# Attention and mixture-of-experts kernel: another order of loads, squares and weight splits in its opening

## The chip, the cores and the metric

The kernel runs on one core of a Trainium2 chip. The core has a matrix engine (TensorE, PE in the profile), a vector engine (VectorE, DVE), an engine for activation functions (ScalarE, ACT), a general engine (GpSimd, POOL) and a synchronisation engine (SyncE, SP) that here issues nearly all DMAs. A name with a q behind it (SPq, POOLq) is the instruction queue of that engine. The metric is the device time of one execution in microseconds.

## The reference

Two stages follow each other. The attention is linear attention with random features, and its output, with the heads put side by side, is the input of four dense experts whose outputs are summed with normalised weights:

```python
def phi(x):                                   # x: (batch 4, heads 8, seq 576, dim 64), omega: (128, 64)
    h = einsum('bhsd,md->bhsm', x, omega) - sum(x * x) / 2
    return exp(h - max(h)) / sqrt(128)
q_p, k_p = phi(q * 64**-0.25), phi(k * 64**-0.25)
kv  = einsum('bhsm,bhsd->bhmd', k_p, v)
num = einsum('bhsm,bhmd->bhsd', q_p, kv)
den = einsum('bhsm,bhm->bhs', q_p, sum_s(k_p)) + 1e-6
x   = (num / den) as (2304, 512)
p   = domain_probs / (sum(domain_probs) + 1e-9)
out = sum over e in 0..3 of p[:, e] * (relu(x @ w1[e]) @ w2[e])       # w1: 512x1024, w2: 1024x512
```

## The kernel before, in words

All is float32 at the borders. The expert matmuls split each operand into a high part in a rounded format (fp32r) and a low part that is the remainder, and use three products: high by high, low by high, high by low.

**Attention.** Heads are worked in pairs, four pairs a batch. For batch 0 (class `Pair`) a pair's keys lie as 64 rows; `square` writes their squares into the other 64 rows of the tile, so that one matmul with `om` (features above, a constant below) gives projection minus half the squared length. `project` makes it for a group of token tiles and takes the row maxima on VectorE, `exp` the exponentials on ScalarE, `sum_keys` sums keys by values into `kv` and copies it out (`kvs`), `turn` transposes the query features, `numerators` multiplies them with `kvs` and divides, `finish` transposes the result into the ring buffers `x_hi` and `x_lo`.

**Experts.** A visit is half an expert for a block of tokens. `hidden` makes four hidden tiles (128 features each) from the rings and four `w1` tiles, `relu` splits them into `hh` and `hl`, `outputs` multiplies them with four `w2` tiles and accumulates. Weights come as raw tiles of 128x512 (`wraw`, 256 KB each): `load_w` issues the next load on SP, `split_w` takes the oldest raw tile, writes its high part (on ScalarE as a rule, on GpSimd in the opening) and its low part (on GpSimd), and then calls `load_w`. A raw tile's buffer is free again once its low part is written. There are `RAWB` raw buffers.

**Order.** The kernel is written with a manual schedule: on each engine the instructions stand in the order of the code, and SP issues DMAs in that order too, so that a DMA that waits for a buffer holds all behind it.

`begin` (L452) is the opening: the first 256 tokens of batch 0 for all four pairs, staggered. While pair 0's keys are summed, pair 1's are projected, and pair 2's and 3's are being loaded and squared. Among them stand the first eight `split_w`, four for `w1` and four for `w2`, and at the end the first expert visit's `hidden`, in four parts as the pairs finish. `first_visit` (L570) does that visit's `relu` and `outputs` with eight more splits, for the second visit, and between its steps `emit` runs `first_rest` (L582), the remaining 320 tokens of batch 0. After that, `steps` runs visits with the other batches' attention between them.

Of the kernel before, what the change touches and what calls it, by code (L numbers as in the profile page):

```python
# [7 lines left out]
F32R = mybir.dt.float32r  # L8
# [6 lines left out]
def attention_moe(ctx, tc, kT, qT, kd, qd, kn, qn, vn, omT, probs, w1, w2, out):  # L15
# [10 lines left out]
    nc = tc.nc  # L26
    _, NP, D, _ = kT.shape
# [3 lines left out]
    E, FT, P, KC, _ = w1.shape  # L31
    EPS = 1e-6
    QS = float(D) ** -0.25
    RING = 1536
# [3 lines left out]
    const = ctx.enter_context(tc.tile_pool(name="const", bufs=1))  # L38
    att = ctx.enter_context(tc.tile_pool(name="att", bufs=2))
    moe = ctx.enter_context(tc.tile_pool(name="moe", bufs=1))  # L40
    psum = ctx.enter_context(tc.tile_pool(name="psum", bufs=8, space=bass.MemoryType.PSUM))

    def bank(name):
        return psum.tile([P, 512], F32, tag="ps", name=name)

    def f32(ap):
        return ap.bitcast(F32)
# [6 lines left out]
    prs = const.tile([P, NT // P], F32, name="prs")  # L54
    vas = [const.tile([P, 4, VW], F32, name=f"va{i}") for i in range(2)]
    vbs = [const.tile([P, NP, VW], F32, name=f"vb{i}") for i in range(2)]
    x_hi = const.tile([P, NP, RING], F32R, name="x_hi")
    x_lo = const.tile([P, NP, RING], F32R, name="x_lo")

    def scale_om():  # L60
        nc.vector.tensor_scalar(om[:D], om[:D], QS, None, ALU.mult)

    def normalize_probs():
        nc.vector.tensor_reduce(prs, pr, AX.X, ALU.add)
        nc.vector.tensor_scalar(prs, prs, 1e-9, None, ALU.add)
        nc.vector.reciprocal(prs, prs)
        nc.vector.tensor_tensor(pr, pr, prs[:, :, None].to_broadcast([P, NT // P, E]), ALU.mult)
# [282 lines left out]
                mine = [(256, 256)] + mine  # L350
            visits.append((u, e, hf, mine))

    W1B, W2B, RAWB, HB, AB = 6, 6, 4, 6, 7
    W = {}
    items = [(v, which, i) for v in range(len(visits)) for which in ("w1", "w2") for i in range(FH)]
    loads, splits = list(items), list(items)
# [2 lines left out]
    def load_w(eng=nc.sync):  # L359
        if not loads:  # L360
            return
        v, which, i = key = loads.pop(0)
        _, e, hf, _ = visits[v]
        f = hf * FH + i
        raw[key] = t = moe.tile([P, 512], F32, tag="wraw", name="wraw", bufs=RAWB)
        eng.dma_start(t, w1[e, f].rearrange("p k f -> p (k f)") if which == "w1" else w2[e, f * P:(f + 1) * P])

    def split_w(hi=nc.scalar, lo=nc.gpsimd):
        if not splits:
            return  # L370
        key = splits.pop(0)
        t = raw.pop(key)
        a, c = (moe.tile([P, 512], F32R, tag=key[1] + x, name=key[1] + x, bufs={"w1": W1B, "w2": W2B}[key[1]]) for x in "hl")
        if hi is nc.scalar:
            hi.activation(a, t, AF.Copy)  # L375
        else:
            hi.tensor_copy(a, t)
        lo.tensor_tensor(c, t, f32(a), ALU.subtract)  # L378
        W[key] = a, c
        load_w()  # L380
# [15 lines left out]
    def relu(ps, n):  # L396
        ha, hc = (moe.tile([P, 512], F32R, tag=x, name=x, bufs=HB)[:, :n] for x in ("hh", "hl"))
        nc.scalar.activation(ha, ps[:, :n], AF.Relu)  # L398
        nc.vector.scalar_tensor_tensor(hc, ps[:, :n], 0.0, f32(ha), ALU.max, ALU.subtract)  # L399
        return ha, hc  # L400

    def outputs(v, hs, i, t):

        _, e, hf, _ = visits[v]
        ps = bank("g2")
        ts_ = slice(t * P, (t + 1) * P)
        for c in range(FH):
            (ha, hc), (wa, wc) = hs[c], W[v, "w2", c]
            nc.tensor.matmul(ps, ha[:, ts_], wa, start=(c == 0), stop=False)  # L409
            nc.tensor.matmul(ps, ha[:, ts_], wc, start=False, stop=False)  # L410
            nc.tensor.matmul(ps, hc[:, ts_], wa, start=False, stop=(c == FH - 1))  # L411
        sc = pr[:, i, e:e + 1]
        n_tiles[i] += 1
        if n_tiles[i] == 1:
            acc[i] = moe.tile([P, DM], F32, tag="acc", name="acc", bufs=AB)
            nc.scalar.activation(acc[i], ps, AF.Copy, scale=sc)
        else:
            nc.vector.scalar_tensor_tensor(acc[i], ps, sc, acc[i], ALU.mult, ALU.add)  # L418
        if n_tiles[i] == len(HALVES):
            stores.append((i, acc.pop(i)))  # L420
# [31 lines left out]
    def begin():  # L452

        ps = [Pair(0, hp) for hp in range(NP)]
        first, rest = slice(0, 4 * P), slice(4 * P, 9 * P)
        ps[0].load("k", [first, rest])
        nc.scalar.dma_start(om[:D], omT)
        ps[0].load("q0", eng=nc.scalar)
        ps[1].load("k", [first, rest])
        nc.gpsimd.memset(om[D:], -QS * QS / 2)  # L460
        ps[1].load("q0", eng=nc.scalar)
        ps[0].load_v()
        make_identity(nc, ident)
        for t in vas[:1]:
            nc.gpsimd.memset(t[:, :, 0:VW:VW - 1], 1.0)
        for t in vbs[:1]:
            nc.gpsimd.memset(t, 0.0)
            nc.gpsimd.memset(t[:D, :, 0:1], 1.0)
            nc.gpsimd.memset(t[D:, :, VW - 1:VW], 1.0)
        ps[0].load_tails()  # L470
        ps[1].load_v()
        load_w()
        load_w()
        scale_om()

        def keys(hp):
            for g in range(3):
                ps[hp].project("k", g)

        def keys_exp(hp):  # L480
            for g in range(3):
                ps[hp].exp("k", g)

        ps[0].square("k", nc.scalar, first)
        ps[0].square("k", nc.vector, rest)
        ps[0].square("q0", nc.scalar)
        ps[1].square("k", nc.scalar, first)
        ps[1].square("k", nc.gpsimd, rest)
        nc.gpsimd.memset(vas[1][:, :, 0:VW:VW - 1], 1.0)
        keys(0)  # L490

        ps[2].load("k")
        ps[2].load("q0")
        ps[0].project("q", 0)
        ps[1].square("q0", nc.vector)
        keys_exp(0)
        keys(1)
        ps[2].square("k", nc.gpsimd, first)
        ps[2].square("k", nc.gpsimd, rest)

        ps[0].sum_keys()
        ps[2].load_v()
        ps[3].load("k")
        ps[3].load("q0")
        load_w()
        load_w()
        ps[0].exp("q", 0)
        ps[1].project("q", 0)
        keys_exp(1)
        ps[2].square("q0", nc.vector)  # L510
        keys(2)
        ps[3].square("k", nc.gpsimd, first)
        ps[3].square("k", nc.gpsimd, rest)
        nc.gpsimd.memset(vbs[1], 0.0)
        nc.gpsimd.memset(vbs[1][:D, :, 0:1], 1.0)
        nc.gpsimd.memset(vbs[1][D:, :, VW - 1:VW], 1.0)

        ps[0].turn(0, nc.vector)
        ps[1].sum_keys()
        ps[3].load_v()  # L520
        nc.sync.dma_start(pr, probs.rearrange("(i p) e -> p i e", p=P))
        ps[1].exp("q", 0)
        ps[2].project("q", 0)
        keys_exp(2)
        ps[3].square("q0", nc.vector)
        keys(3)
        for _ in range(4):
            split_w(nc.gpsimd, nc.gpsimd)
        for p in ps[:2]:
            p.load("q1")  # L530
        for j in range(2):
            nc.sync.dma_start(om_r[j * D:(j + 1) * D], omT)

        ps[0].numerators(0)
        ps[1].turn(0, nc.vector)
        ps[2].sum_keys()
        ps[2].exp("q", 0)
        ps[3].project("q", 0)
        keys_exp(3)
        for p in ps[:2]:  # L540
            p.square("q1", nc.gpsimd)
        for _ in range(4):
            split_w(nc.gpsimd, nc.gpsimd)

        ps[0].finish(0)
        ps[1].numerators(0)
        ps[2].turn(0, nc.vector)
        ps[3].sum_keys()
        ps[3].exp("q", 0)

        normalize_probs()
        nc.vector.tensor_scalar(om_r, om_r, QS, None, ALU.mult)
        ps[1].finish(0)
        ps[2].numerators(0)
        ps[3].turn(0, nc.vector)
        g1 = [bank("g1") for _ in range(FH)]
        for f in range(FH):
            hidden(0, f, 0, 256, g1[f], [0])
        ps[2].finish(0)
        ps[3].numerators(0)  # L560
        for f in range(FH):
            hidden(0, f, 0, 256, g1[f], [1])
        ps[3].finish(0)
        for f in range(FH):
            hidden(0, f, 0, 256, g1[f], [2])
        for f in range(FH):
            hidden(0, f, 0, 256, g1[f], [3])
        return ps, g1

    def first_visit(g1):  # L570
        hs = []
        for f in range(FH):
            split_w()
            hs.append(relu(g1[f], 256))
            yield 0.5
        for t in range(2):
            for _ in range(2):
                split_w()
            outputs(0, hs, t, t)
            yield 1  # L580

    def first_rest(pairs):  # L582
# [101 lines left out]
```

## Time and profile before

| | us |
|---|---|
| median of 3 runs (lowest to highest) | 975.51 (974.34 to 976.88) |
| the profiled execution | 980.6 |
| its span, first to last instruction | 978.2 |
| TensorE busy in the span | 957.4 |

The profiled execution is 5.1 us longer than the median, and 2.4 us of it lie outside the span. All that follows is read from that one execution. Times in a timeline are microseconds from the start of the span. The granted clock is a share of full speed: 1.00 is 2.4 GHz, 0.50 is 1.2 GHz, and a value between is a stretch with both.

### The profile page before, as it was taken

The page shows a single profiled execution, that of the slowest core. Times are in us where ns is not written, and L with a number is a line of the kernel's source. Part 1 is how long each engine was busy: PE and PEld are TensorE (multiplying, and loading weights), DVE is VectorE, ACT ScalarE, POOL GpSimd, SP SyncE. Part 2 cuts the span into 40 slices and gives each one's busy share as a digit, 9 for nine tenths or more (in the row PEclk, how much of TensorE's full clock was granted, in tenths as well). Part 3 has the DMA queues.
Part 4 walks back from the last instruction along what each step waited for, and adds up shares of the span by engine and source line. Part 5 has one row for each costly group of instructions (what it writes and reads, how often), then busy time and mean ns, then how long its engine had stood idle before and what let it go on. Part 6 is the DMA issues. An engine that isn't in the chain of part 4 may idle for free.

```text
span 978.2 us, 13669 instructions
## 1 busy us (share of the span) xinstructions
PE 957.4 (98%) x5216; PEld 808.6 (83%) x5216; DVE 369.2 (38%) x760; ACT 342.2 (35%) x806; POOL 371.8 (38%) x312
## 2 busy tenths in 40 slices
PE   6989999999999999999999999999999999999998
PEld 6978888887888888878888888888888888888887
DVE  3434445553334444343333354544311222222222
ACT  3345344433262324334326252434323221322120
POOL 3756543343342234444444344444414422431230
PEclk9799999999999999999999999999999999999999
DMA  6434544232432412423263342422313211221211
GB/s 152 108 107 119 171 126 135 78 111 80 126 89 80 141 48 86 145 69 90 82 202 99 112 135 76 135 78 75 109 63 86 76 34 64 87 65 31 78 33 65
DMA packets 60737, 94.09 MB, mean 96 GB/s; under 512 B 10176, under 2 KB 18560, under 8 KB 60672
## 3 DMA queue, kind: packets, MB, share of 16 engines
q1 hardware_dynamic: 60432, 92.92, 32.4%
q8 instruction: 41, 0.67, 0.3%
q10 hardware_dynamic: 240, 0.30, 0.1%
q14 instruction: 24, 0.20, 0.1%
HBM read 88.48 MB, written 4.72 MB: 95 GB/s over the span
## 4 chain that ended last, share of the span: by engine, by line
PE 94%; ACT 2%; DMA 1%; DVE 1%; POOL 1%; SPq 1%; issue 0%; POOLq 0%; ACTq 0%
PE g L392 14%; PE g L394 14%; PE g L393 14%; PE g L409 13%; PE g L411 13%; PE g L410 13%; PE kv L142 3%; PE nd L166 2%; PE qt_ps L151 2%; PE k_ps L234 1%; PE q_ps L234 1%; PE x_ps L188 1%; PE t_ps L238 1%; DMA k<-in_kT 1%; DMA va<-in_vn 1%; PE k_ps L114 1%
## 5 line engine op out<-in xcount | busy, mean ns | idle before, releaser
L378 POOL TENSOR_TENSOR w1l<-wraw,w1h 128x512 fp32r<-128x512 f32 x128 | 164.5, 1286 | 383.5 <-ACT w1h L375 374.9
L392 PE MATMUL g<-x_hi,w1h 128*128 128x512 f32 (+1 forms) x688 | 252.8, 367 | 0.0
L394 PE MATMUL g<-x_hi,w1l 128*128 128x512 f32 (+1 forms) x688 | 248.0, 360 | 0.0
L393 PE MATMUL g<-x_lo,w1h 128*128 128x512 f32 (+1 forms) x688 | 247.9, 360 | 0.0
L399 DVE SCALAR_TENSOR_TENSOR hl<-g,hh 128x512 fp32r<-128x512 f32 (+1 forms) x172 | 104.1, 605 | 345.4 <-ACT hh L398 345.4
L409 PE MATMUL g<-w2h,hh 128*128 128x512 f32 x576 | 228.4, 397 | 0.2 <-ACT hh L398 0.2
L411 PE MATMUL g<-w2h,hl 128*128 128x512 f32 x576 | 225.5, 391 | 0.0
L410 PE MATMUL g<-w2l,hh 128*128 128x512 f32 x576 | 225.0, 391 | 0.0
L398 ACT ACTIVATE hh<-g 128x512 fp32r<-128x512 f32 (+1 forms) x172 | 91.0, 529 | 375.0 <-PE g L394 374.8
L378 POOL TENSOR_TENSOR w2l<-wraw,w2h 128x512 fp32r<-128x512 f32 x128 | 163.1, 1289 | 144.0 <-ACT w2h L375 143.4
L418 DVE SCALAR_TENSOR_TENSOR acc<-g,pr,acc 128x512 f32<-128x512 f32 x126 | 94.6, 750 | 192.9 <-PE g L411 192.5
L394 PEld LDWEIGHTS g<-x_hi,w1l 128*128 128x128 f32 x688 | 131.0, 190 | 21.0
L392 PEld LDWEIGHTS g<-x_hi,w1h 128*128 128x128 f32 x688 | 131.1, 190 | 20.7 <-issue 0.5
L393 PEld LDWEIGHTS g<-x_lo,w1h 128*128 128x128 f32 x688 | 131.1, 190 | 19.5
L411 PEld LDWEIGHTS g<-w2h,hl 128*128 128x128 f32 x576 | 108.2, 188 | 24.1 <-DVE hl L399 1.1
L409 PEld LDWEIGHTS g<-w2h,hh 128*128 128x128 f32 x576 | 108.4, 188 | 23.5 <-ACT hh L398 0.7
L410 PEld LDWEIGHTS g<-w2l,hh 128*128 128x128 f32 x576 | 108.3, 188 | 21.3
L375 ACT ACTIVATE w2h<-wraw 128x512 fp32r<-128x512 f32 x124 | 76.2, 635 | 104.2 <-PE g L411 55.1
L375 ACT ACTIVATE w1h<-wraw 128x512 fp32r<-128x512 f32 x124 | 77.8, 627 | 0.1
L265 ACT ACTIVATE kp<-k_ps,nbk 128x128 f32<-128x128 f32 x96 | 27.4, 379 | 34.1 <-DVE nbk L259 34.1
L166 PEld LDWEIGHTS nd<-kvs,qt 128*128 128x128 f32 x256 | 33.9, 196 | 3.5 <-DVE qt L157 1.5
L166 PE MATMUL nd<-kvs,qt 128*128 128x65 f32 x256 | 33.0, 273 | 1.4 <-DVE qt L157 1.4
(82 smaller groups left out, 599.4 us busy)
## 6 DMA issues: line engine op xcount, KB each, us to landing
wraw<-in_w SPq DMA_DIRECT2D x256, 256.0 KB, 2.7
out<-acc SPq DMA_DIRECT2D x18, 256.0 KB, 3.2
va<-in_vn SPq DMA_DIRECT2D x16, 256.0 KB, 5.5
k<-in_kd SPq DMA_DIRECT2D x12, 288.0 KB, 3.1
q<-in_qd SPq DMA_DIRECT2D x12, 288.0 KB, 4.6
k<-in_kn SPq DMA_DIRECT2D x12, 288.0 KB, 4.9
q<-in_qn SPq DMA_DIRECT2D x12, 288.0 KB, 5.2
q<-in_qT SPq DMA_DIRECT2D x4, 160.0 KB, 3.4
```

The source lines that it names most:

```text
L166: nc.tensor.matmul(nd[:, t, cs], self.query_tile(j, 2 * part + t), self.kv[:, cs], start=True, stop=True)
L375: hi.activation(a, t, AF.Copy)
L378: lo.tensor_tensor(c, t, f32(a), ALU.subtract)
L392: nc.tensor.matmul(ps[:, :n], wa[:, w], x_hi[:, k, cs], start=(k == 0), stop=False)
L393: nc.tensor.matmul(ps[:, :n], wa[:, w], x_lo[:, k, cs], start=False, stop=False)
L394: nc.tensor.matmul(ps[:, :n], wc[:, w], x_hi[:, k, cs], start=False, stop=(k == KC - 1))
L398: nc.scalar.activation(ha, ps[:, :n], AF.Relu)
L399: nc.vector.scalar_tensor_tensor(hc, ps[:, :n], 0.0, f32(ha), ALU.max, ALU.subtract)
L409: nc.tensor.matmul(ps, ha[:, ts_], wa, start=(c == 0), stop=False)
L410: nc.tensor.matmul(ps, ha[:, ts_], wc, start=False, stop=False)
L411: nc.tensor.matmul(ps, hc[:, ts_], wa, start=False, stop=(c == FH - 1))
L418: nc.vector.scalar_tensor_tensor(acc[i], ps, sc, acc[i], ALU.mult, ALU.add)
```

## The change

Five things change.

1. The first two weight loads move behind pair 2's keys and queries in SP's order, and pair 2's keys are loaded in two pieces (512 and 640 columns) instead of one.
2. The squares of pair 2's first piece move from GpSimd to VectorE, ahead of pair 1's maxima; the second piece stays on GpSimd.
3. There are six raw weight buffers instead of four. As many loads are issued ahead as before (four), so a load no longer waits for the low part that was just issued, but for the one two splits earlier.
4. In `first_visit` each `relu` stands ahead of its split and each `outputs` ahead of its two splits, and six of the eight low parts go to VectorE (the four of `w1`, and one of two after each `outputs`).
5. `x_hi` and `x_lo` are allocated from a pool of their own behind the others.

```diff
+    xs = ctx.enter_context(tc.tile_pool(name="xs", bufs=1))
...
+    x_hi = xs.tile([P, NP, RING], F32R, name="x_hi")
+    x_lo = xs.tile([P, NP, RING], F32R, name="x_lo")
...
-    x_hi = const.tile([P, NP, RING], F32R, name="x_hi")
-    x_lo = const.tile([P, NP, RING], F32R, name="x_lo")
...
-    W1B, W2B, RAWB, HB, AB = 6, 6, 4, 6, 7
+    W1B, W2B, RAWB, HB, AB = 6, 6, 6, 6, 7
...
         ps[1].load_v()
-        load_w()
-        load_w()
         scale_om()
...
         keys(0)
-        ps[2].load("k")
+        ps[2].load("k", [first, rest])
         ps[2].load("q0")
+        load_w()
+        load_w()
         ps[0].project("q", 0)
         ps[1].square("q0", nc.vector)
         keys_exp(0)
+        ps[2].square("k", nc.vector, first)
         keys(1)
-        ps[2].square("k", nc.gpsimd, first)
         ps[2].square("k", nc.gpsimd, rest)
...
         for f in range(FH):
-            split_w()
             hs.append(relu(g1[f], 256))
+            split_w(lo=nc.vector)
             yield 0.5
         for t in range(2):
-            for _ in range(2):
-                split_w()
             outputs(0, hs, t, t)
+            split_w()
+            split_w(lo=nc.vector)
             yield 1
```

The instructions below are listed in the order in which they stand on an engine; line numbers of the changed kernel are two higher from L92 on. First SP in the opening, before: `k` of 1152 columns are pair 2's and then pair 3's keys, `q` their queries, `va` values, `wraw` weights.

```order
L94 DMA va_73<-in_vn 128x4x128
L366 DMA wraw<-in_w 128x512 x2
L90 DMA k<-in_kT 64x1152
L90 DMA q_135<-in_qT 64x512
L94 DMA va_72<-in_vn 128x4x128
L90 DMA k<-in_kT 64x1152
L90 DMA q_192<-in_qT 64x512
L366 DMA wraw<-in_w 128x512 x2
```

The same place on SP in the changed kernel:

```order
L96 DMA va_78<-in_vn 128x4x128
L92 DMA k<-in_kT 64x512
L92 DMA k<-in_kT 64x640
L92 DMA q_135<-in_qT 64x512
L368 DMA wraw<-in_w 128x512 x2
L96 DMA va_77<-in_vn 128x4x128
L92 DMA k<-in_kT 64x1152
L92 DMA q_196<-in_qT 64x512
L368 DMA wraw<-in_w 128x512 x2
```

Pair 2's keys are now directly behind pair 1's values; pair 3's keys stand where they stood, behind the values that take pair 0's buffer.

VectorE in the opening, before; `q_90` are pair 1's queries, the `nm` after it the maxima of pair 1, and the last two rows the first of pair 2.

```order
L117 TENSOR_REDUCE nm<-q_ps 128x4
L106 TENSOR_TENSOR q_90<-q_90 64x512
L117 TENSOR_REDUCE nm<-k_ps 128x4 x2
L117 TENSOR_REDUCE nm<-k_ps 128x1
L117 TENSOR_REDUCE nm<-q_ps 128x4
L106 TENSOR_TENSOR q_135<-q_135 64x512
L117 TENSOR_REDUCE nm<-k_ps 128x4 x2
```

The same place on VectorE in the changed kernel:

```order
L119 TENSOR_REDUCE nm<-q_ps 128x4
L108 TENSOR_TENSOR q_93<-q_93 64x512
L108 TENSOR_TENSOR k<-k 64x512
L119 TENSOR_REDUCE nm<-k_ps 128x4 x2
L119 TENSOR_REDUCE nm<-k_ps 128x1
L119 TENSOR_REDUCE nm<-q_ps 128x4
L108 TENSOR_TENSOR q_135<-q_135 64x512
L119 TENSOR_REDUCE nm<-k_ps 128x4 x2
```

The square of pair 2's first piece stands ahead of pair 1's maxima, which so wait for that piece's landing.

VectorE in `first_visit`, before; `g` are the four hidden tiles, `nm<-q_ps` the maxima of the remaining queries of pairs 0 and 1, `qt` the copies after `turn` of pair 0.

```order
L399 SCALAR_TENSOR_TENSOR hl<-g_485,hh 128x256
L117 TENSOR_REDUCE nm<-q_ps 128x4
L117 TENSOR_REDUCE nm<-q_ps 128x1
L399 SCALAR_TENSOR_TENSOR hl<-g_486,hh 128x256
L117 TENSOR_REDUCE nm<-q_ps 128x4
L117 TENSOR_REDUCE nm<-q_ps 128x1
L399 SCALAR_TENSOR_TENSOR hl<-g_487,hh 128x256
L399 SCALAR_TENSOR_TENSOR hl<-g_488,hh 128x256
L157 COPY qt<-qt_ps 128x512
```

The same place on VectorE in the changed kernel, from the second hidden tile on:

```order
L380 TENSOR_TENSOR w1l<-wraw,w1h 128x512
L119 TENSOR_REDUCE nm<-q_ps 128x4
L119 TENSOR_REDUCE nm<-q_ps 128x1
L401 SCALAR_TENSOR_TENSOR hl<-g_490,hh 128x256
L380 TENSOR_TENSOR w1l<-wraw,w1h 128x512
L119 TENSOR_REDUCE nm<-q_ps 128x4
L119 TENSOR_REDUCE nm<-q_ps 128x1
L401 SCALAR_TENSOR_TENSOR hl<-g_491,hh 128x256
L380 TENSOR_TENSOR w1l<-wraw,w1h 128x512
L401 SCALAR_TENSOR_TENSOR hl<-g_492,hh 128x256
L380 TENSOR_TENSOR w1l<-wraw,w1h 128x512
L159 COPY qt<-qt_ps 128x512
```

Behind each `hl` now stands a low part of `w1`, so four of them are ahead of the copies that pair 0's numerators read.

## Rows read from the trace of the kernel before

**Rows 1.** Stretches of TensorE: length, busy us (instructions), granted clock, DMA share, GB/s.
```profile
20.00:30.00 10.00, 9.50 (x46) 0.51 0.27 66
...
40.00:50.00 10.00, 10.00 (x64) 0.66 0.37 107
...
60.00:70.00 10.00, 7.17 (x38) 0.90 0.59 163
70.00:80.00 10.00, 10.00 (x74) 0.93 0.29 89
80.00:978.20 898.20, 890.62 (x4783) 1.00 0.32 94
```

**Rows 2.** Waits of TensorE, first 80 us: total us, times, longest.
```profile
PE k_ps L114 <- POOL k L106: 4.0, 2, 3.5
PE qt_ps L151 <- ACT qp L126: 2.8, 1, 2.8
```

**Rows 3.** Timeline of SP's queue, first 42 us: start, us, instruction, count.
```profile
11.05 0.98 SPq L366 DMA_DIRECT2D wraw<-in_w  x2
12.20 0.48 SPq L90 DMA_DIRECT2D k<-in_kT  x1
...
15.25 0.47 SPq L90 DMA_DIRECT2D k<-in_kT  x1
...
33.59 1.11 SPq L90 DMA_DIRECT2D q<-in_qT  x2
```

**Rows 4.** Landing times of the key loads, first 40 us.
```profile
DMA to landing us min/median/max: 2.9/5.0/6.5
```

**Rows 5.** Timeline of GpSimd, VectorE and ScalarE around pair 2's keys.
```profile
11.53 0.69 DVE L106 TENSOR_TENSOR q<-q 64x512 f32<-64x512 f32 x1
...
12.24 1.49 DVE L117 TENSOR_REDUCE nm<-k_ps 128x4 f32<-128x512 f32 x3
...
15.95 2.46 ACT L126 ACTIVATE kp<-k_ps,nm 128x128 f32<-128x128 f32 x9
...
18.13 2.69 POOL L106 TENSOR_TENSOR k<-k 64x512 f32<-64x512 f32 x2 [4.36 <-DMA k<-in_kT]
18.77 0.94 DVE L106 TENSOR_TENSOR q<-q 64x512 f32<-64x512 f32 x1 [2.36 <-DMA q<-in_qT]
...
21.88 2.25 POOL L106 TENSOR_TENSOR k<-k 64x512 f32<-64x512 f32 x2 [1.06 <-DMA k<-in_kT]
```

**Rows 6.** Timeline of TensorE, 14 to 40 us.
```profile
14.57 1.11 PE L114 MATMUL q_ps<-om,q 128*128 128x128 f32 x8
19.21 1.16 PE L114 MATMUL k_ps<-om,k 128*128 128x128 f32 x8 [3.54 <-POOL k L106]
...
24.45 3.52 PE L142 MATMUL kv<-va,kp 128*128 128x65 f32 x16
...
29.57 2.62 PE L114 MATMUL k_ps<-om,k 128*128 128x128 f32 x18
...
33.54 1.90 PE L142 MATMUL kv<-va,kp 128*128 128x65 f32 x16
...
36.44 1.00 PE L166 MATMUL nd<-kvs,qt 128*128 128x65 f32 x8
37.27 0.61 PE L151 MATMUL qt_ps<-ident,qp 128*128 128x128 f32 x4
39.15 0.49 PE L138 MATMUL kv<-vb,kp 128*128 128x130 f32 x2 [1.27 <-ACT kp L126]
```

**Rows 7.** The page's group of `w1` low parts on GpSimd.
```profile
L378 POOL TENSOR_TENSOR w1l<-wraw,w1h 128x512 fp32r<-128x512 f32 x128 | 164.5, 1286 | 383.5 <-ACT w1h L375 374.9
```

**Rows 8.** Timeline of ScalarE, 48 to 90 us.
```profile
63.66 0.63 ACT L375 ACTIVATE w2h<-wraw 128x512 fp32r<-128x512 f32 x1 [3.68 <-DMA wraw<-in_w]
...
67.26 1.40 ACT L126 ACTIVATE qp<-q_ps,nm 128x128 f32<-128x128 f32 x5
```

**Rows 9.** Timeline of SP's queue, 48 to 90 us.
```profile
60.86 7.30 SPq L366 DMA_DIRECT2D wraw<-in_w  x6
```

## Prediction

> **What bounds the kernel now.** I read TensorE by stretches first. After 80 us it is busy for 890.6 of 898.2 us at the full clock [rows 1]; none of the edits touches that work, so what they are worth lies in the first 80 us. There the reader sees two kinds of loss. The first is a lower clock: 10 x (1 - 0.51) = 4.9 us between 20 and 30, 10 x (1 - 0.66) = 3.4 between 40 and 50, and 1.0 + 0.7 = 1.7 between 60 and 80 [rows 1]. The second is waiting, read next: 4.0 us for GpSimd's squares of pair 2's keys and 2.8 for ScalarE's exponentials of pair 1's late queries [rows 2], and 1.3 for ScalarE's exponentials of pair 3's keys [rows 6]. Each fall of the clock follows one of these waits, so a wait that goes may take a low stretch with it. Last I read who was late at each wait, on the timelines.
>
> **First piece: pair 2's keys.** Their load was issued at 12.20, behind two weight loads from 11.05 [rows 3], and GpSimd could square only at 18.13 [rows 5], 5.9 us later. TensorE had ended its work before at 14.57 + 1.11 = 15.7 and started these keys at 19.21 [rows 6]. Now the load takes the weights' place at 11.05, in two pieces 0.6 apart. The traced landings are 2.9 to 6.5 us, median 5.0 [rows 4]; that gives 14.0 to 17.6 for the first piece. I take 15.0, a landing of 4: the piece is under half of the load that took 5.9, and 512 KB less stands before it. VectorE squares it in 0.69 [rows 5] to 15.7, just as TensorE is free. The second piece lands at 15.6 and takes GpSimd 640/1152 of 2.25 = 1.25 [rows 5], to 16.9; TensorE asks for it at 16.7. So the wait of 4.0 becomes about 0.2 (bounds: 0, and 2.6 if the first piece lands at 17.6).
>
> VectorE is in order, so pair 1's three maxima (1.49 from 12.24) stand behind that square, from 15.7 to 17.2. For them waits ScalarE: its exponentials of pair 1's keys started at 15.95 and took 2.46 [rows 5]; now the first maximum is there at 16.4 and they end at 18.9. TensorE comes to pair 1's key sum at 16.9 + 1.3 for ten more projections + 0.5 for a turn = 18.7. Cost 0.2.
>
> **What is late next: pair 3's keys.** Their load keeps its issue at 15.25 [rows 3], since it stands behind a values load that waits for pair 0's key sum, and the bytes ahead of it are the same. I leave its landing at 21.88. GpSimd's squares take 2.25 for both pieces [rows 5], the first (512/1152 of it) to 22.9, the second to 24.1. TensorE at full clock: the key sum 1.90 [rows 6] and 0.3 for its first matmul, from 18.9 to 21.1, query projection 1.1 to 22.2. It waits 0.7 there and 0.2 more for the second piece, and ends pair 3's keys at 24.1 + 1.3 = 25.4 instead of 29.57 + 2.62 = 32.2 [rows 6]. **Gain 6.8 us.** Most of it is the first low stretch: the same sixteen key-sum matmuls took 3.52 low and 1.90 high [rows 6].
>
> **From there to the first visit.** Pair 2's key sum ended at 33.54 + 1.90 = 35.4, and pair 3's started at 39.15 after a wait of 1.27 [rows 6]. The 3.7 us between are ScalarE's chain from one sum to the next (copy, query exponentials, nine key exponentials), which no edit touches. The wait stays, and I keep the low stretch of 3.4 us behind it. So this part moves 6.8 us earlier as a whole, and gains nothing more.
>
> GpSimd's opening splits do not bind: they may start as before, and the two late queries' loads at 33.59 stood behind four weight loads [rows 3], two of which now have a free buffer. The weight loads that moved back have over 10 us until their splits.
>
> **First visit.** ScalarE waited 3.68 us for a raw weight tile [rows 8], in front of pair 1's late exponentials at 67.26; SP took 7.30 us to issue the six loads there [rows 9], each held by a low part just issued. With six buffers, six of eight low parts (7.7 us by 1.286 each [rows 7]) off GpSimd and `outputs` ahead of its splits, I see those tiles there some 5 us before they are read, and the 2.8 us wait goes. New waits take its place. On VectorE four low parts stand ahead of pair 0's copies. The trace has none on VectorE; bounds are 0.69, the two-input square of 512 columns [rows 5], and 1.29 as on GpSimd [rows 7]; I take 0.69, the same engine and width. They are 2.8 us, of which TensorE's twelve output matmuls hide all but 0.4 (at 1.29: 2.8 not hidden). Pair 1's five exponentials (1.40 [rows 8]) still come behind two splits and a copy: 1.1 not hidden. Net 2.8 - 1.5 = **1.3 us gained**, and, the 1.1 being spread over five transposes, the low stretch's **1.7** too.
>
> Beside the GpSimd squares VectorE's square took 0.94 instead of 0.69, and GpSimd's pair 2.69 instead of 2.25 [rows 5]: together 0.7 lost, one whole VectorE instruction. The Trainium skill (SBUF — State Buffer, SBUF: two separate sides) says that a VectorE instruction with two SBUF inputs and a GpSimd instruction that reads SBUF shut each other out for a whole instruction; the trace's sum agrees. By it one of the four low parts could wait 1.25 us behind GpSimd's query square, and the gain would be 1.2 us smaller; by the row, 0.3.
>
> The new pool only changes addresses: no instruction comes or goes. I take 0, and no row prices it.
>
> **Sum.** 6.8 + 1.3 + 1.7 = 9.8 us of the profiled execution: 980.6 becomes 970.8. The median of the runs is 5.1 below that execution, so I subtract from it: 975.5 - 9.8 = 965.7. Where those 5.1 us lie is not known; if some were in these waits, the gain is smaller.
>
> **Rivals.**
> - *The clock falls at the new wait for pair 3's keys and stays low.* For it: a wait of 1.27 was enough at 39 us, and key sums and numerators at the low clock did not bring it back between 20 and 30 [rows 1]. Against: 0.7 + 0.2 in pieces is shorter. From 24.1 on all then doubles. Up to pair 3's key sum that is 1.3 of projections, numerators 0.8 (36.44 to 37.27), turn 0.6, key sum 2.2, query projection 1.1, a transpose 0.2, numerators 0.8 and turn 0.6 [rows 6], 7.6 us; the sum then starts at 24.1 + 2 x 7.6 = 39.3, as it did. The first gain is 0 at worst, which leaves the first visit's 3.0: 972.5; half of it if the clock returns midway: 969.
> - *No fall before pair 3's key sum either.* The 3.4 us go too: 962.3. For it: only 1.27 us of waiting caused that fall; against: the same work leads up to it.
> - *Pair 2's keys land hardly sooner* (a landing of 5.9 or more from 11.05, set by the transfers of values and the next loads rather than by the weights). TensorE still waits over 2 us, the clock falls as before, and only the 1.15 us of earlier issue and the first visit's 3.0 remain: 971.3.
> - *VectorE's low parts cost what they do on GpSimd.* First visit gives 0.6 instead of 3.0: 968.1.
> - *Slower:* the clock falls at the wait for pair 3's keys and the first hidden matmuls do not bring it back either. A low stretch costs half its length. Before, the two up to 50 us cost 4.9 + 3.4 and the two waits there 4.0 + 1.3, 13.6 in all; now it is half of the one low stretch plus 1.1 of new waits. With the first visit's 3.0 in hand the change is slower from a low stretch of 2 x (13.6 + 3.0 - 1.1) = 31 us on; one from 24 to 61, through all of the first visit's hidden matmuls, gives 18.5 + 1.1 - 16.6 = 3.0 more, 978.5. Against: between 40 and 50 the clock did come back within the stretch [rows 1].
>
> The Trainium skill (TensorE: Matmul & The Clock Gate, The HAM clock gate) says that the monitor is not restarted with a kernel, so one kernel's clock changes fall differently from run to run; one traced execution cannot show that.
>
> **How the numbers follow.** Forecast 0.44; no fall at pair 3's sum 0.17; low clock from pair 3's keys 0.22; keys hardly sooner 0.09; low parts dear 0.04; slower 0.04. About 0.3% (2.9 us) is what a measurement of this kernel can tell from no change: faster is below 972.6. Faster gets the forecast, the second rival, most of the others that stay below 972.6: 0.83; same 0.13, half of the low clock at its worst and some of the late keys; slower 0.04. The range runs from 962 (the second rival) to 973.5 (the low clock at its worst and 1 us for a late first piece).
>
> **What would show it.** Right: pair 2's projections start by 16.5 us with a wait under 0.5; the granted clock stays 1.00 between 20 and 30; pair 3's keys end near 25 with a wait for GpSimd's square under 1; ScalarE no longer waits for a raw tile near 60; pair 1's late exponentials start some 9 us before 67.26 [rows 8]. Wrong: a low stretch that starts near 24 and lasts beyond 30, a first wait of over 2 us at pair 2's keys, or VectorE's low parts above 1 us each with TensorE waiting for a `qt` copy. After 80 us of before, nothing should differ.

## The result: 1.5% faster, more than forecast

| | before | after |
|---|---|---|
| median, us (lowest to highest) | 975.41 (974.34 to 976.88), 4 runs | 960.31 (959.87 to 962.85), 4 runs |
| profiled execution | 980.6 | 959.87 |
| its span | 978.2 | 958.0 |

The ratio is 0.985 (95% interval 0.9828 to 0.9871). The forecast was 965.7 with a range from 962; the time lies below it. Of the experiments below, the profiled executions of visit_only (granted clock 0.56 throughout) and of the first keys3_early (5,367 us) were disturbed as a whole; their traces are not read, and the ratios leave those two executions out (the medians do not).

TensorE by stretches in the changed kernel, in the columns of [rows 1]:

```profile
20.00:30.00 10.00, 8.44 (x74) 1.00 0.64 151
...
40.00:50.00 10.00, 10.00 (x70) 1.00 0.38 106
60.00:70.00 10.00, 10.00 (x73) 1.00 0.36 112
70.00:80.00 10.00, 9.06 (x65) 1.00 0.38 106
80.00:958.00 878.00, 871.02 (x4707) 1.00 0.31 94
```

No stretch is at the low clock any more. The waits of TensorE in the first 80 us answer [rows 2]: GpSimd's squares now cost 1.6 us instead of 4.0, and the 2.8 us for ScalarE's `qp` are gone.

```profile
PE k_ps L116 <- POOL k L108: 1.6, 2, 1.1
PE kv L140 <- ACT kp L128: 1.3, 1, 1.3
PE x_ps L190 <- DVE xt L175: 1.3, 2, 0.9
```

The opening came out almost to the tenth, in part by luck: pair 3's keys landed 0.56 us sooner than assumed (21.32 for 21.88), and GpSimd's squares of them took 2.69 instead of 2.25. SP's queue (against [rows 3]), and then the other engines (against [rows 5, 6]):

```profile
10.94 1.11 SPq L92 DMA_DIRECT2D k<-in_kT  x2
...
12.73 1.06 SPq L368 DMA_DIRECT2D wraw<-in_w  x2
...
14.72 0.47 SPq L92 DMA_DIRECT2D k<-in_kT  x1
```

```profile
14.25 0.68 DVE L108 TENSOR_TENSOR k<-k 64x512 f32<-64x512 f32 x1 [3.22 <-DMA k<-in_kT]
...
14.98 1.25 POOL L108 TENSOR_TENSOR k<-k 64x640 f32<-64x640 f32 x1 [1.38 <-DVE k L108]
...
14.99 2.68 PE L116 MATMUL k_ps<-om,k 128*128 128x128 f32 x18
...
21.32 2.69 POOL L108 TENSOR_TENSOR k<-k 64x512 f32<-64x512 f32 x2 [5.09 <-DMA k<-in_kT]
...
22.41 1.16 PE L116 MATMUL k_ps<-om,k 128*128 128x128 f32 x8 [1.06 <-POOL k L108]
...
24.07 1.38 PE L116 MATMUL k_ps<-om,k 128*128 128x128 f32 x10 [0.50 <-POOL k L108]
...
32.43 0.49 PE L140 MATMUL kv<-vb,kp 128*128 128x130 f32 x2 [1.28 <-ACT kp L128]
...
32.75 1.90 PE L144 MATMUL kv<-va,kp 128*128 128x65 f32 x16
```

Pair 2's projections start at 14.99 with no wait; pair 3's keys land at 21.32 (forecast 21.88), cost waits of 1.06 and 0.50 (0.7 and 0.2), and end at 24.07 + 1.38 = 25.45 (25.4). The wait before pair 3's key sum is still there (1.28), but its sixteen matmuls behind it took 1.90 us, the full-clock time: here the clock did not fall.

The first visit, VectorE and ScalarE (against [rows 7, 8]):

```profile
43.70 0.69 DVE L380 TENSOR_TENSOR w1l<-wraw,w1h 128x512 fp32r<-128x512 f32 x1
...
51.80 1.82 DVE L380 TENSOR_TENSOR w2l<-wraw,w2h 128x512 fp32r<-128x512 f32 x1 [1.68 <-ACT w2h L377]
...
55.89 1.35 DVE L380 TENSOR_TENSOR w2l<-wraw,w2h 128x512 fp32r<-128x512 f32 x1 [1.15 <-ACT w2h L377]
...
56.08 1.40 ACT L128 ACTIVATE qp<-q_ps,nm 128x128 f32<-128x128 f32 x5
```

VectorE's low part of `w1` takes 0.69, as assumed, those of `w2` 1.82 and 1.35; ScalarE waits for no raw tile, and pair 1's late exponentials start at 56.08 instead of 67.26.

What was not forecast comes later. The first `hh` (high part of a hidden tile) of the second visit, of before and then of after:

```profile
71.71 0.38 ACT L398 ACTIVATE hh<-g 128x256 fp32r<-128x256 f32 x1 [3.05 <-PE g L394]
```

```profile
59.33 0.38 ACT L400 ACTIVATE hh<-g 128x256 fp32r<-128x256 f32 x1 [1.85 <-PE g L396]
```

There the changed kernel is 12.4 us ahead; at the end of the span 20.2. **So 7.8 us came after the second visit's start, where the same instructions run at the full clock.** They are in the matmuls of `hidden`. One line of them between 760 and 930 us, before and after (count of 512 columns | busy us, mean ns):

```profile
L392 PE MATMUL g<-x_hi,w1h 128*128 128x512 f32 x80 | 31.7, 397 | 0.0
```

```profile
L394 PE MATMUL g<-x_hi,w1h 128*128 128x512 f32 x88 | 34.2, 389 | 0.0
```

Matmuls overlap, so the rate is read from starts. 24 matmuls of `outputs` begin, then a block of 48 of `hidden`, then the next `outputs`, before and after:

```profile
902.04 0.40 PE L409 MATMUL g<-w2h,hh 128*128 128x512 f32 x1
...
907.50 0.40 PE L392 MATMUL g<-x_hi,w1h 128*128 128x512 f32 x1
...
918.75 0.39 PE L409 MATMUL g<-w2h,hh 128*128 128x512 f32 x1
```

```profile
882.51 0.40 PE L411 MATMUL g<-w2h,hh 128*128 128x512 f32 x1
...
887.98 0.39 PE L394 MATMUL g<-x_hi,w1h 128*128 128x512 f32 x1
...
898.86 0.39 PE L411 MATMUL g<-w2h,hh 128*128 128x512 f32 x1
```

For `hidden` that is 11.25 / 48 = 234 ns before and 10.88 / 48 = 227 ns after, 7.7 ns less (0.37 us over 48). For `outputs` it is 5.46 / 24 and 5.47 / 24, 228 ns in both. The three lines of `hidden` hold 116 groups of four matmuls of 512 columns each: 3 x 116 x 4 = 1392, by 7.7 ns some 11 us. Over all 1330 pairs of such matmuls that follow each other behind 80 us the mean distance of starts is 234.0 before and 227.7 after: 6.3 ns, or 8.8 us.

### The profile page after: what moved, and what is told of

Same layout as the page of the kernel before. It is cut to its first block, busy times and chain, and to the rows that moved or that the text cites. A ratio compares the mean times of both kernels' runs of the same rounds, so it can differ in the third digit from the quotient of the medians.

```text
span 958.0 us, 13688 instructions
## 1 busy us (share of the span) xinstructions
PE 941.4 (98%) x5216; PEld 798.2 (83%) x5216; DVE 373.6 (39%) x767; ACT 342.5 (36%) x806; POOL 363.3 (38%) x305
## 4 chain that ended last, share of the span: by engine, by line
PE 94%; ACT 2%; DMA 1%; DVE 1%; POOL 0%; SPq 0%; issue 0%; POOLq 0%; ACTq 0%
PE g L411 14%; PE g L394 14%; PE g L413 14%; PE g L412 14%; PE g L396 14%; PE g L395 13%; PE kv L144 3%; PE nd L168 2%; PE qt_ps L153 2%; PE k_ps L236 1%; PE q_ps L236 1%; PE t_ps L240 1%; PE x_ps L190 1%; DMA k<-in_kT 1%; DMA va<-in_vn 1%; ACT hh L400 0%
## 5 line engine op out<-in xcount | busy, mean ns | idle before, releaser
L380 POOL TENSOR_TENSOR w1l<-wraw,w1h 128x512 fp32r<-128x512 f32 x124 | 159.6, 1288 | 381.8 <-ACT w1h L377 368.7
L394 PE MATMUL g<-x_hi,w1h 128*128 128x512 f32 (+1 forms) x688 | 249.1, 362 | 0.0
L396 PE MATMUL g<-x_hi,w1l 128*128 128x512 f32 (+1 forms) x688 | 244.6, 355 | 0.0
L395 PE MATMUL g<-x_lo,w1h 128*128 128x512 f32 (+1 forms) x688 | 244.1, 355 | 0.0
L380 POOL TENSOR_TENSOR w2l<-wraw,w2h 128x512 fp32r<-128x512 f32 x126 | 161.0, 1292 | 147.5 <-ACT w2h L377 146.9
L394 PEld LDWEIGHTS g<-x_hi,w1h 128*128 128x128 f32 x688 | 130.1, 189 | 18.4 <-issue 0.5
```

The lines of the kernel that those rows point to most:

```text
L394: nc.tensor.matmul(ps[:, :n], wa[:, w], x_hi[:, k, cs], start=(k == 0), stop=False)
L395: nc.tensor.matmul(ps[:, :n], wa[:, w], x_lo[:, k, cs], start=False, stop=False)
L396: nc.tensor.matmul(ps[:, :n], wc[:, w], x_hi[:, k, cs], start=False, stop=(k == KC - 1))
```

## The experiments

Ratios are to the kernel before in the same set of runs, with 95% intervals.

### Which part gives the time

**ring_only**: before with the rings in their own pool.

```diff
-    x_hi = const.tile([P, NP, RING], F32R, name="x_hi")
-    x_lo = const.tile([P, NP, RING], F32R, name="x_lo")
+    x_hi = xs.tile([P, NP, RING], F32R, name="x_hi")
+    x_lo = xs.tile([P, NP, RING], F32R, name="x_lo")
```

> Only the ring buffers move to a pool behind the others. Theory A (the place of the rings sets the length of the hidden matmuls of 512 columns, 234 ns from start to start in the trace of before and 227 in the trace after, some 1390 of them): 8 to 10 us faster, 966 us, with the opening unchanged (wait for GpSimd's squares 4.0 us, low clock between 20 and 30). Theory B (the place is worth nothing, the whole gain of 15.1 us is the opening's): 975 us, within 1 us.

**opening_only**: the changed kernel with the rings back in `const` (the reverse of that diff), run in two sets.

> The changed kernel with the rings put back among the constants: all edits of order, loads and splits, not the pool. Theory A: 968 to 970 us, the opening worth 6 to 7 us in the timed runs, hidden matmuls of 512 columns at 234 ns. Theory B: 960 us. The prediction's own sum for these edits was 965.7 with one fall of the clock kept, 962.3 without it.

> All edits but the rings' pool once more. Theory G: 968 to 970, at or above the run before. Theory H: 1 to 3 us below the run before, 965 to 967.

**keys_only**: before with edits 1 and 2 alone, still four raw tiles.

```diff
-        load_w()
-        load_w()
...
-        ps[2].load("k")
+        ps[2].load("k", [first, rest])
         ps[2].load("q0")
+        load_w()
+        load_w()
...
+        ps[2].square("k", nc.vector, first)
         keys(1)
-        ps[2].square("k", nc.gpsimd, first)
```

> Only the weights' first loads behind pair 2's keys and their squares shared between VectorE and GpSimd. By the prediction 6.8 us faster (968.7), pair 3's projections ending near 25.5 us, and the 2.8 us wait for pair 1's late exponentials left as it was. Rival: the first visit is bound by GpSimd's splits and raw tiles, which are no earlier, so the wait there grows and gives most of it back: 973 or more.

**visit_only**: before with edits 3 and 4 alone (`RAWB` 6, and the diff of `first_visit`).

> Only six raw weight tiles and the first visit's order with its low parts on VectorE. By the prediction 3.0 us faster (972.5), the 2.8 us wait and the low stretch after it gone, the opening up to 53 us unchanged. Rival: with the opening as late as before, weights were early enough anyhow and the low parts on VectorE delay the copies: 975, no change.

| | median, us | ratio |
|---|---|---|
| ring_only | 966.39 | 0.9913 (0.99 to 0.9926) |
| opening_only | 970.44, 968.45 | 0.9942 (0.9925 to 0.9958), 0.9942 (0.9923 to 0.996) |
| keys_only | 975.05 | 1.0 (0.9989 to 1.001) |
| visit_only | 972.35 | 0.9966 (0.9956 to 0.9976) |

The rings' place alone gives 8.5 us, more than all that the prediction priced gives together (5.7, by the ratio of opening_only). The keys alone give nothing measurable. In keys_only pair 3's keys end early, at 21.44 + 2.59 = 24.0, and yet:

```profile
25.54 6.03 SPq L366 DMA_DIRECT2D wraw<-in_w  x4
...
32.78 1.23 SPq L532 DMA_DIRECT2D om_r<-in_omT  x2
```

```profile
37.38 0.98 DVE L552 TENSOR_SCALAR om_r<-om_r 128x128 f32<-128x128 f32 x1 [3.45 <-DMA om_r<-in_omT]
```

```profile
39.50 0.44 PE L188 MATMUL x_ps<-ident,xt 128*128 128x128 f32 x2 [3.11 <-DVE xt L173]
```

The load of `om_r`, another tile of features, stands on SP behind weight loads that GpSimd's low parts hold back. VectorE waits 3.45 us for it, and the `xt` queued behind comes 3.11 late to TensorE. The time won by the keys is lost again there: the first late query projection (of the 320 remaining tokens) starts at 47.15, and at 47.26 in a second execution of before (before_again, below), whose keys ended at 26.5.

### Where the rings must lie

Three explanations were open: an alignment of the ring, the streamed operand, by itself; the region of memory; or where ring and weight tile stand to each other. Each of the following runs moves addresses alone, by an unused tile.

**pad_ahead, pad_behind**: before with 32 bytes ahead of, or behind, the rings. **after_pad**: the changed kernel with 32 bytes ahead of the rings in their pool.

```diff
+    pad = const.tile([P, 8], F32, name="pad")
     x_hi = const.tile([P, NP, RING], F32R, name="x_hi")
     x_lo = const.tile([P, NP, RING], F32R, name="x_lo")
```

> The kernel before with a tile of 32 bytes ahead of the rings, so that the rings and all behind them start 32 bytes later: the rings' addresses go from a multiple of 64 bytes to an odd multiple of 32, the weights' from an odd multiple of 32 to a multiple of 64. Theory A (a streamed operand that starts at a multiple of 64 bytes costs 234 ns at 512 columns, one at an odd multiple of 32 costs 227): hidden matmuls 227, output matmuls 234 instead of 227, their 1700 taking back what the 1392 hidden ones give, so 975 to 978 us. Theory B (the low region of the memory is slow, or something that lies beside the rings there): hidden 234, outputs 227, 975.5. Theory C (streamed and resident operand must have the same alignment): hidden 234, outputs 227, 975.5. Theories B and C are told apart by the next run.

> The kernel before with the same 32 bytes behind the rings: the rings stay at a multiple of 64 bytes, the weights and hidden tiles go to one as well. Theory A (streamed operand at a multiple of 64 is slow): hidden 234 and outputs 234, 12 us slower, 987. Theory B (region): hidden 234, outputs 227, 975.5. Theory C (same alignment of both operands): hidden 227, outputs 227, 967.

> The changed kernel with 32 bytes ahead of the rings in their pool, which puts the rings, still at the end of the memory, back at a multiple of 64 bytes; nothing else moves. Theories A and C: hidden matmuls back at 234 ns, 969 us. Theory B (region): 227 ns and 960 us as in the changed kernel.

**pad_1184, pad_160, pad_928**: before with so many bytes behind the rings (296, 40 and 232 columns of float32).

> The kernel before with 1184 bytes between the rings, which stay where they are, and all that lies behind them. New theory D: a hidden matmul is fast when its two operands, ring and weight tile, start at the same address modulo 2048 bytes. So it is in the changed kernel and in the one with the rings moved alone (both 992), and in every output matmul; in the kernel before the difference was 864, with 32 bytes ahead of the rings 864, behind them 896, with 32 in the changed kernel's pool 2016, all slow. The 1184 bytes make it 0 with the rings still in the low region: D expects 227 ns and 966 us. Rival E (the place of the rings at the memory's end and at 32 bytes more than a multiple of 64 must both hold): 234 ns and 975 us.

> The same with 160 bytes: the difference is 1024 bytes modulo 2048. D with 2048 as the modulus expects 234 ns and 975 us; D with a modulus of 1024 or a smaller power of two above 128 expects 227 ns and 966 us; rival E 975.

> The kernel before with 928 bytes behind the rings, so that the high weight tiles stand 1792 bytes from the ring's blocks modulo 2048 (0 modulo 256, but 256 modulo 512). If the modulus by which ring and weight tile must agree is 256, the hidden matmuls of 512 columns go from 234 to 227 ns and the time to about 967 us. If it is 512 or 1024, they stay at 234 ns and the time at about 975 us. The other theory, that any place but the old one is fast, also expects 227; the 928 bytes can't tell it from the first, and the 32 bytes already spoke against it.

The first column is the distance from a ring block to a high weight tile of `w1`, modulo 256 bytes, worked out from the sizes in allocation order (ring blocks and weight tiles both repeat at multiples of 2048 bytes):

| | distance mod 256 | hidden matmul, ns | median, us | ratio |
|---|---|---|---|---|
| before | 96 | 234 | 975.41 | |
| pad_ahead | 96 | 234 | 975.33 | 1.0001 (0.9984 to 1.0018) |
| pad_behind | 128 | 233 | 974.22 | 0.9994 (0.9979 to 1.0009) |
| after_pad | 224 | 233 | 966.62 | 0.9922 (0.9895 to 0.995) |
| after | 0 | 227 | 960.31 | 0.985 (0.9828 to 0.9871) |
| ring_only | 0 | 227 | 966.39 | 0.9913 (0.99 to 0.9926) |
| pad_1184 | 0 | 227 | 967.02 | 0.9915 (0.9899 to 0.993) |
| pad_160 | 0 | 227 | 968.9 | 0.9931 (0.9917 to 0.9945) |
| pad_928 | 0 | 227 | 968.33 (one run) | |

The same block of 48 matmuls, in pad_behind and in pad_928:

```profile
901.94 0.40 PE L393 MATMUL g<-x_hi,w1h 128*128 128x512 f32 x1
...
913.13 0.39 PE L410 MATMUL g<-w2h,hh 128*128 128x512 f32 x1
```

```profile
896.46 0.39 PE L393 MATMUL g<-x_hi,w1h 128*128 128x512 f32 x1
...
907.34 0.39 PE L410 MATMUL g<-w2h,hh 128*128 128x512 f32 x1
```

11.19 against 10.88. Alignment by itself is ruled out: pad_ahead moves the rings by 32 bytes and changes nothing. The region is ruled out twice: pad_1184 is fast in the old region, after_pad slow in the new. What holds over nine kernels is that the fast ones have a distance of 0 modulo 256; 128 does not do. pad_1184 and pad_160 agree modulo 1024 too, pad_928 only modulo 256. All operands of `outputs` have distance 0, in every kernel, and its matmuls are always at 227 to 228.

The traces give the price a second time. From the second visit's first `hh` to the end it is 898.6 to 899.6 us in the seven readable traces with distance 0, 906.4 to 907.7 in the ten with 96 or 128, and 904.6 in after_pad.

Two limits remain. The unused tiles move the rings against everything that is allocated behind them, the attention's tiles too; that the weight tile is the partner is concluded from its being the matmul's other operand, and from the rate near 907 us, where in before no attention instruction has run since 840. And why the chip behaves so was not shown; distances other than 0, 96, 128 and 224 were not tried.

### Was the traced execution of before typical?

**before_again**: the kernel before, unchanged, profiled once more.

> The kernel before once more, for a second trace of its opening. If the low stretch between 20 and 30 us is a matter of the single execution (the run with the rings moved alone has the same opening code, waited 2.3 us for GpSimd's squares, and had none), this trace ends pair 3's projections near 26 us and runs about 975; if it belongs to the kernel, near 32 and 980.

It took 976.14 us (span 974.3). TensorE by stretches, and pair 3's projections:

```profile
15.00:20.00 5.00, 3.12 (x16) 0.72 0.94 241
20.00:30.00 10.00, 10.00 (x90) 0.97 0.41 96
30.00:40.00 10.00, 8.71 (x56) 0.71 0.34 94
```

```profile
24.32 2.17 PE L114 MATMUL k_ps<-om,k 128*128 128x128 f32 x18
```

The stretch from 20 to 30 had 0.51 in [rows 1] and 0.97 here; pair 3's keys end at 26.5, not at 32.2 [rows 6]. The second visit's first `hh` comes at 66.74 instead of 71.71, 5.0 us earlier: that is about the 5.1 by which the first execution exceeded the median. Between 30 and 40 this execution has a low stretch of its own, behind the wait for pair 3's keys, which costs 10 x (1 - 0.71) = 2.9 us and another 0.5 up to 41 (granted clock 0.95 between 40 and 50).

The two are not the whole spread. In all eight traces with the opening of before (these two, ring_only and the five with an unused tile in `const`) pair 3's keys end at 26.1 to 32.2 us, in five of them at 28.0 to 29.3, and the first late query projection starts at 46.9 to 52.9.

### What the raw tiles and the first visit's order do

**raw6_only**: before with `RAWB` 6 and nothing else. **keys_raw6** (two sets): keys_only with `RAWB` 6.

```diff
-    W1B, W2B, RAWB, HB, AB = 6, 6, 4, 6, 7
+    W1B, W2B, RAWB, HB, AB = 6, 6, 6, 6, 7
```

> Only six raw weight tiles instead of four. Theory F (the six tiles are what lets the other edits count: they free SP's queue, and alone they end the wait for raw tiles in the first visit): 973 to 974, with ScalarE's 3 to 4 us wait for a raw tile near 60 us shorter. Rival (they only matter together with the earlier keys): 975.4.

> The weights' first loads behind pair 2's keys and the shared squares, with six raw weight tiles; first visit and rings as before. The run with four raw tiles gained nothing (975.0) and showed why: SP's loads of the feature matrix stood behind weight loads that waited for GpSimd, VectorE's scaling of it waited 3.45 us, and TensorE 3.1 us behind that. If that wait is what took the gain back, six raw tiles give 971 to 972.5 and a wait of under 0.5 us there. Rival (the squares' wait was no loss at all, since ScalarE's chain sets the pace behind it): 975 still, with the wait gone from there and put elsewhere.

> The earlier keys with six raw tiles once more, on the same chip as the next run. Theory G (the first visit's new order and VectorE's low parts give nothing, or cost a little, once the six tiles are there): the same as the next run or up to 2 us faster. Theory H (they give 1 to 3 us as the prediction had it, and the difference between the two earlier runs, 967.9 and 970.4, came from how soon the keys landed on either chip): slower than the next run by that.

raw6_only 971.51, ratio 0.996 (0.9946 to 0.9975); keys_raw6 967.93, 0.9922 (0.9907 to 0.9937), and 967.23, 0.9919 (0.9906 to 0.9931). By these ratios the keys gave 0 on four raw tiles, and 7.7 - 3.9 = 3.8 us on six. visit_only, which is raw6_only with the new order of `first_visit`, gave no more than raw6_only (0.9966). In keys_raw6 SP reaches `om_r` 3.2 us earlier than in keys_only, and VectorE no longer waits for it:

```profile
29.59 1.23 SPq L532 DMA_DIRECT2D om_r<-in_omT  x2
```

```profile
35.12 0.21 DVE L552 TENSOR_SCALAR om_r<-om_r 128x128 f32<-128x128 f32 x1
```

keys_raw6 is the changed kernel's opening with neither the new order of `first_visit` nor VectorE's low parts, and it is not slower than opening_only, which has them: 967.23 against 968.45 in the same set, with intervals that overlap. Nor would those 1.2 us be the new order's alone, since pair 3's keys were also squared sooner in keys_raw6 (see the end). The traces isolate it better. The stretch from the first late query projection to the second visit's first `hh`, from the traces:

```
before 18.8   before_again 19.5   ring_only 17.8   keys_only 18.4
pad_ahead, pad_1184, pad_160, pad_928           17.5 to 17.7   pad_behind 18.6
raw6_only, keys_raw6 (both), best               14.4
opening_only (both), after, after_pad, keys3_early_2   15.6 to 15.7
```

Six tiles shorten it by 3.1 to 5.1 us (from 18.4 to 14.4 with the new keys); the new order, with its low parts on VectorE, gives 1.3 back. VectorE in keys_raw6, second set, and in opening_only, second set, where pair 0's late numerators are divided:

```profile
51.87 0.17 DVE L170 TENSOR_SCALAR r<-nd 128x6 f32<-128x6 f32 x1 [1.47 <-PE nd L168]
```

```profile
51.94 1.70 DVE L378 TENSOR_TENSOR w2l<-wraw,w2h 128x512 fp32r<-128x512 f32 x1 [1.69 <-ACT w2h L375]
53.56 0.15 DVE L170 TENSOR_SCALAR r<-nd 128x6 f32<-128x6 f32 x1
```

A low part of `w2` stands there ahead of `r` and holds it 1.7 us. It takes 1.70 (1.82 in the changed kernel) instead of 0.69 while GpSimd's own low part runs beside it. The Trainium skill (SBUF — State Buffer, SBUF: two separate sides) has a VectorE instruction with two SBUF inputs and a GpSimd instruction that reads SBUF shut each other out for a whole instruction. The trace of the changed kernel agrees: GpSimd's starts at 51.79 and takes 1.29, VectorE's starts at 51.80 and ends 0.54 behind GpSimd's, where alone it takes 0.69.

The held `r` is not all of the 1.3. TensorE waits only 0.20 us for the `xt` made from it, and ScalarE too has another order: two high parts of `w2` now stand ahead of pair 1's late exponentials. These start 12.5 us after the first late query projection in opening_only, second set, and 11.2 after it in keys_raw6, second set:

```profile
54.88 1.14 ACT L375 ACTIVATE w2h<-wraw 128x512 fp32r<-128x512 f32 x2
...
56.24 1.40 ACT L126 ACTIVATE qp<-q_ps,nm 128x128 f32<-128x128 f32 x5
```

```profile
55.53 1.40 ACT L126 ACTIVATE qp<-q_ps,nm 128x128 f32<-128x128 f32 x5
```

No run has the order without the low parts on VectorE, so what each costs stays open.

### Two steps further

**keys3_early** (two sets): the changed kernel with pair 3's keys loaded right behind pair 2's first queries.

```diff
         ps[2].load("q0")
+        ps[3].load("k")
         load_w()
...
-        ps[3].load("k")
         ps[3].load("q0")
```

> The changed kernel with pair 3's keys loaded directly behind pair 2's queries, ahead of the first weights and of the values for pair 2. The changed kernel waits 1.06 and 0.50 us for GpSimd's squares of pair 3's keys, which land at 21.3. If that wait sets the end, 1.3 to 1.6 us go: 959. Rival (ScalarE's exponentials of pair 2's keys, which end at 24.1, or the values that now load later hold pair 2's key sum): 960.3, as it is, with a longer wait at that key sum.

> The changed kernel with pair 3's keys loaded earlier once more, for its trace. Expected 958 to 959 against the changed kernel's 960.3, with no wait for GpSimd's squares of pair 3's keys, and pair 3's projections ending near 24 us. If the gain of the first time was the chip's, 960.3.

958.64, ratio 0.9829 (0.9813 to 0.9845), and 958.89, 0.9837 (0.9824 to 0.9849): some 1.5 us below the changed kernel by the medians, with intervals that overlap.

**best**: that, with `first_visit` as before.

```diff
+            split_w()
             hs.append(relu(g1[f], 256))
-            split_w(lo=nc.vector)
...
+            for _ in range(2):
+                split_w()
             outputs(0, hs, t, t)
-            split_w()
-            split_w(lo=nc.vector)
```

> The changed kernel with two edits on top: pair 3's keys loaded right behind pair 2's first queries, and the first visit's order and its engines for the low parts as in the kernel before. If the first visit's new order costs time on the late path, as its stretch from the first late query projection to the second visit shows (15.7 us against 14.4), the runs add up: six raw tiles with the new keys gave 0.9919 and 0.9922, the rings' place 0.9913, pair 3's earlier keys some 1.5 us, together 0.9920 x 0.9913 less 0.0015 = 0.982, 957.5 us or, by the 1.3 us of the late path on pair 3's early keys alone, 958.7 less 1.3 = 957.4. Rival: the low parts on VectorE pay once the rings are in their place, since other work then stands beside them; then it is no faster than the changed kernel with pair 3's early keys (0.983 to 0.984, 958.8 us) or slower, 960.

957.14 us (956.28 to 959.95), ratio 0.9828 (0.9807 to 0.9848), the lowest median of all. The trace shows both gains: the stretch above is 14.4, and pair 3's keys end at 23.6 without a wait (25.45 with two waits in the changed kernel):

```profile
21.41 2.17 PE L116 MATMUL k_ps<-om,k 128*128 128x128 f32 x18
```

By the ratios alone it can't be told from keys3_early; its own forecast of 957.4 to 957.5 held.

## Why the prediction was wrong

**"The new pool only changes addresses ... I take 0".** This is the step that failed. Nothing in a trace of before prices an address, and the prediction put one value where it had no bound. It is worth 8.5 us by ring_only and 7.8 by the two traces, about half of the 15.1 us gained. Without it (opening_only) the time lies inside the range, at 970.4 and 968.5. "After 80 us of before, nothing should differ" fell with it. That `hidden` and `outputs` have matmuls of the same shape at 234 and 228 ns stood in the starts of before; the prediction did not compare them.

**"Gain 6.8 us".** Its end point was right (25.45 for 25.4), its start was not the kernel's: 32.2 belongs to one execution with a long low stretch. Against before_again it is 26.5 - 25.45 = 1.0, against the five traces near 28 to 29 it is 2.6 to 3.9. Taken off the median, as the sum did, 6.8 was too much; the prediction named this doubt and did not act on it.

**"The wait stays, and I keep the low stretch".** The wait stayed (1.28 for 1.27); the low stretch behind it comes in some executions only. ring_only and the changed kernel have the same wait and, behind it, the same sixteen matmuls at 3.07 and 1.90 us:

```profile
33.09 0.49 PE L140 MATMUL kv<-vb,kp 128*128 128x130 f32 x2 [1.27 <-ACT kp L128]
33.42 3.07 PE L144 MATMUL kv<-va,kp 128*128 128x65 f32 x16
```

Three of the changed kernel's four runs have a mean granted clock of 1.0 and 959.87 to 960.49 us, the fourth 0.996 and 962.85. From pair 3's projections to the first late query before_again took 20.8 us and the changed kernel 18.2: 2.6 less, of the 2.9 + 0.5 that its low stretch there costs. That is the second rival's mechanism. The Trainium skill (TensorE: Matmul & The Clock Gate, The HAM clock gate) lets a kernel's clock changes fall differently from run to run. The two executions of before agree: 0.51 and 0.97 between 20 and 30, 0.98 and 0.71 between 30 and 40.

**First visit, 1.3 + 1.7 = 3.0.** Against before_again it gave 19.5 - 15.7 = 3.8. The size is near, the reasons are not: six raw tiles do all of it and more, while the new order with low parts on VectorE costs 1.3. The prediction counted `w1`'s four low parts in front of the copies, which were hidden, and not the low part of `w2` in front of pair 0's divisions. The conflict with GpSimd that it feared for `w1` came there.

**"GpSimd's opening splits do not bind".** For the change this held: with six raw tiles VectorE scales `om_r` at 35.88 without a wait. On four raw tiles they do bind (keys_only): through SP's order they hold `om_r`. So edits 1 and 2 paid only together with edit 3, while edit 3 paid 3.9 us alone (raw6_only).

The sum against before_again: keys 1.0, no fall 2.6 and first visit 3.8 make 7.4 up to the second visit's first `hh`, and 8.9 come behind it, 0.8 of these because before_again was at the low clock up to 68.4. Together that is 16.3, the difference of the two spans (974.3 - 958.0); the medians differ by 15.1. A single pair of traces can't split the gain more finely, since the opening varies between executions. Over the eight traces with the old opening the first late query projection starts at 49.1 us in the mean, over the four with the new one (after, after_pad, opening_only twice) at 45.2, and the first visit's stretch shrinks from 18.2 to 15.7: 3.9 + 2.5 = 6.4.

opening_only gives 5.7 by its ratio: six of its twelve executions took 970.4 to 972.0 us at a mean granted clock of 0.994 to 0.998, the other six 966.5 to 968.9 at 0.996 to 1.0.

## What to carry to other kernels

Compare the start-to-start times of matmuls of one shape across a kernel's stages: a stage that is slower by a few per cent at the same clock may be paying for where its tiles lie, and unused tiles of several sizes test that (32 bytes did not help here, 160 did). Profile the unchanged kernel more than once before a low-clock stretch is booked as a gain. An edit that makes one load earlier is worth what the next load in the same queue allows, so price it together with what holds that queue.

## What the hardware showed unexpectedly

- A 512-column fp32r matmul of this kernel starts every 227 ns when its streamed ring block and its weight tile are 0 apart modulo 256 bytes, and every 233 to 234 ns at 96, 128 and 224: 3% of these matmuls' time, 8.5 us of 975. The mechanism is open.
- The same wait of 1.27 to 1.28 us of TensorE was followed by the low clock in one execution and not in another of nearly the same instructions.
- VectorE's low part of 512 columns takes 0.69 us alone and 1.35 to 1.82 beside GpSimd's.

Left open: GpSimd starts pair 3's squares at 20.4 and 19.9 us in the two traces of keys_raw6 and at 22.4 and 21.5 in those of opening_only, whose openings are written alike.
